# Router gates on GpSimd, a shared tail tile for two batches, and a new instruction order in a fused pooled-attention and mixture-of-experts kernel

## The chip, the cores and the metric

The kernel runs on one core of one Trainium2 chip. A core has five engines that run side by side, each through its own queue in order: PE (TensorE, matmuls and transposes into PSUM), DVE (VectorE), ACT (ScalarE), POOL (GpSimd, which also issues the casting loads) and SP (SyncE, which issues DMAs). PSUM has eight banks. The metric is the device time of one execution in microseconds.

## What is computed

Eight batches; q, k and v of shape (8 batches, 8 heads, 576 tokens, 64), float32. First an attention whose keys and values are means over 8 neighbouring tokens (72 pooled keys); its output, 512 wide, goes into four experts, each a causal attention over 576 tokens with head width 64. A router gives each token the two experts with the largest logits.

```python
k_p = k.reshape(B, H, Sp, pool, D).mean(axis=3)
...
attn = np.exp(scores)
attn = attn / (np.sum(attn, axis=-1, keepdims=True) + 1e-09)
x = attn @ v_p                      # then (B, S, H * D)
...
logits = x @ w_gate
topk = np.argpartition(-logits, K, axis=-1)[..., :K]      # K = 2
w = np.exp(sel); w /= w.sum(-1, keepdims=True) + 1e-09
for e in range(E):
    a = softmax(causal(scale * (x @ wq[e]) @ (x @ wk[e]).T))
    out += mask_e * w_e * (a @ (x @ wv[e]) @ wo[e])
```

## The kernel before

Everything is unrolled: the program is a list of short tokens, SEQ, and each token calls one small function that issues one step for one batch. `S00:3@2` is "scores of expert pair 0, key tile group 0, batch 3, into PSUM bank 2"; a trailing `d` puts a copy on DVE (otherwise ACT), and a trailing `p` on a `y` puts its store off to a later `zs` token. Each engine runs its instructions in the order of the list, and a semaphore is waited for wherever data or a buffer requires it. The list was made by a planner; the kernel's text holds only its result, so the place of a token is the plan's order of time.

The steps of one batch, with capitals for PE and small letters for the engine that empties the bank:

- `L` loads q, k or v (line 126, POOL, cast to bf16; three buffers each), `u` transposes q (298, DVE), `PK`/`kc`/`kt` pool the keys, `PV`/`vc` the values.
- `E` and `e` are scores and exps of the pooled attention (331, ACT), `D`, `d`, `x` the sums and their inverse by log and exp (350 and 354, ACT), `O` and `o` the weighted values into xT (368 and 377, DVE).
- `V` and `v` make the experts' values and the router's logits L (copies at 212); `P` and `p` queries and keys; `S` and `s` the causal scores and their exps into etb (497 and 503, ACT); `a` zeroes the diagonal blocks above the diagonal (512 and 520, POOL).
- `g0` to `g9` make the gates: exp of the logits (ACT), a tournament of maxima and minima for the second largest logit, a mask, the sum and its inverse (415 to 445, DVE).
- `B` multiplies etb with the values and a column of ones; `bz`, `bg` and `b` (555, 557, 562, DVE) take the reciprocal, multiply it with the gate and scale the product into osc. `T`/`t` transposes osc through PE, `F` through a DMA on SP, into oT.
- `Y` and `y` give 128 finished tokens (copies into ofin at 212, ACT or DVE; nine ofin buffers); `zs` stores them from SP (lines 621 and 625).

576 tokens are four tiles of 128 and a tail of 64. Two batches of a pair share one place for their tails (`place` 4), so that xT, the values and the outputs of two tails stand in one tile of 128. The B step isn't shared: each batch has products of 128 rows for its tail, half of them unused, as a part of its own (batches 0, 1, 6, 7) or in a part with a main tile (batches 2 to 5, three tiles wide). W0, W1, W2, W3 and W4 load the weights of query, key, value, router and output.

Of the kernel before, what the change touches and what calls it, by code (L numbers as in the profile page):

```python
# [16 lines left out]
ISEQ = mybir.AluOpType.is_equal  # L17
EXP = mybir.ActivationFunctionType.Exp
# [3 lines left out]
def kernel(  # L22
# [65 lines left out]
    ECOLS = 1664  # L88
# [5 lines left out]
    oscs = bufs(4, [128, NTC, 128], BF16, "osc")  # L94
# [100 lines left out]
    def setup_pads():  # L195
        nc.vector.memset(qks[0][:, :, :, S:SPAD], 0.0)
        nc.vector.memset(qks[1][:, 1, :, MAIN - 64 : MAIN], 0.0)
        for t in vaugs:
            nc.vector.memset(t[:, :, :, HD : HD + 1], 1.0)
        for t in etbs:  # L200
            nc.vector.memset(t[:, :, :, 1600:ECOLS], 1.0)
        for h in range(2):
            nc.vector.memset(etbs[1 - h][64 * h : 64 * h + 64, :, :, 1536:1600], 0.0)
# [183 lines left out]
    def small(b, nm, *shape):  # L387
        if (b // 2, nm) not in at:
            at[b // 2, nm] = gtp.tile([128, NPC, *shape], FP32, name=nm, tag=nm)
        return at[b // 2, nm]  # L390
# [6 lines left out]
    def gate(b, step):  # L397
# [11 lines left out]

        if step == 0:  # L410
            nc.scalar.activation(out=tmp("Ex", E), in_=L, func=EXP)
        elif step == 1:
            L2 = L.rearrange("p c (a b) -> p c a b", b=2)
            for nm, op in (("hi", MAXOP), ("lo", MINOP)):
                nc.vector.tensor_tensor(
                    out=tmp(nm, 2, 1), in0=L2[:, :, :, 0:1], in1=L2[:, :, :, 1:2], op=op
                )
        elif step == 2:
            for nm, src, op in (("s2", "hi", MINOP), ("s3", "lo", MAXOP)):
                nc.vector.tensor_tensor(  # L420
                    out=tmp(nm, 1), in0=got(src)[:, :, 0, :], in1=got(src)[:, :, 1, :], op=op
                )
        elif step == 3:
            nc.vector.tensor_tensor(
                out=tmp("m2", 1), in0=got("s2"), in1=got("s3"), op=MAXOP
            )
        elif step == 4:
            nc.vector.tensor_tensor(
                out=tmp("msk", E), in0=L, in1=got("m2").to_broadcast([128, n, E]), op=ISGE
            )  # L430
        elif step == 5:
            nc.vector.tensor_mul(out=tmp("W", E), in0=got("Ex"), in1=got("msk"))
        elif step == 6:
            nc.vector.tensor_add(
                out=tmp("d2", 2), in0=got("W")[:, :, 0:2], in1=got("W")[:, :, 2:4]
            )
        elif step == 7:
            nc.vector.scalar_tensor_tensor(
                out=tmp("den", 1), in0=got("d2")[:, :, 0:1], scalar=1e-9,
                in1=got("d2")[:, :, 1:2], op0=ADD, op1=ADD,  # L440
            )
        elif step == 8:
            nc.vector.reciprocal(out=tmp("rden", 1), in_=got("den"))
        else:
            nc.vector.tensor_mul(
                out=tmp("G", E), in0=got("W"), in1=got("rden").to_broadcast([128, n, E])
            )
# [88 lines left out]
    def Bv(b, bank, ep, part):  # L536
        p0, p1 = span(b, part)
        for e in range(2):
            for i in range(p1 - p0):
                qc = 4 if p0 + i == 4 else p0 + i - 5 * (b % 2)  # L540
                for c in range(qc + 1):
                    col = EOFF[c] + (qc - c) * 128 - (64 if qc == 4 and b % 2 else 0)
# [3 lines left out]
    def osc(b, ep):  # L546
        return oscs[2 * (b % 2) + ep]

    def bv(b, bank, step, ep, part):
        p0, p1 = span(b, part)  # L550
        own = slice(p0 - 4 * (b % 2), p1 - 4 * (b % 2))
        n = p1 - p0
        o, rz, gt = av(b, bank, part), rzbs[ep][:, :, own, :], gts[ep][:, :, own, :]
# [7 lines left out]
        else:  # L561
            nc.vector.tensor_tensor(  # L562
                out=osc(b, ep)[:, own, :].rearrange("p c (e d) -> p e c d", e=2),
# [5 lines left out]
    def T(b, bank, ep, part=None):  # L569
        p0, p1 = span(b, part) if part is not None else (4 * (b % 2), 4 * (b % 2) + NTC)  # L570
        for i in range(p1 - p0):
            flip(half_bank(bank)[:, 128 * i : 128 * i + 128], osc(b, ep)[:, p0 - 4 * (b % 2) + i, :])

    def t(b, bank, dve, ep, part=None):
        o, oT = b % 2, oTs[2 * (b // 2 % 2) + ep]
        if part is None:
            c0, n, at_ = S * o, S, 64 * o
        else:
            p0, p1 = span(b, part)
            c0, n, at_ = (MAIN + 64 * o, TAIL, 64 * o) if p0 == 4 else (128 * p0, 128 * (p1 - p0), 0)  # L580
        copy(dve, oT[:, c0 : c0 + n], half_bank(bank)[:, at_ : at_ + n])


    def crossbar(b, ep, tail):
        oT, own = oTs[2 * (b // 2 % 2) + ep], osc(b, ep)
        if tail:
            nc.sync.dma_start(out=oT[:, tcols(b)], in_=own[half(b), 4 * (1 - b % 2), :], transpose=True)
        else:
            c = b % 2
            nc.sync.dma_start(out=oT[:, mcols(b)].rearrange("p (c n) -> p c n", n=128), in_=own[:, c : c + 4, :].rearrange("p c n -> p (c n)"), transpose=True)  # L590
# [26 lines left out]
    def z(b, c, queue):  # L617
# [16 lines left out]
        u00:0 L_v1:0 r1:0d w1:0 L_v2:0 u01:0 PK0:0@0 W0:0 kc0:0 PK1:0@1 W1:0 kt0:0d E0:0@24 kc1:0 u10:0 L_k0:1 kt1:0  # L634
        H1:0@0 H1:0@0 e00:0 H1:0@0 L_k1:1 u11:0 H1:0@0 H1:0@0 e01:0 N:0 L_k2:1 E1:0@02 L_q0:1 e10:0 E2:0@46 H1:0@0c
        H1:0@0c H1:0@0c L_q1:1 H1:0@0c e21:0 e20:0 e11:0 D2:0@4 D0:0@5 L_q2:1 PV:0@6 d0:0 D1:0@7 vc:0d H1:0@0 x0:0
        c0:0d L_q3:1 d2:0 O00:0@6 d1:0 c1:0d O20:0@5 O01:0@4 o00:0 O10:0@2 x1:0 O11:0@3 o01:0 x2:0 X0:0@0 W2:0 o10:0
        X1:0 o11:0 X2:0 W3:0 c2:0d X3:0 c3:0d o20:0 P_k0:0@4 L_v0:1 h0:0 P_t0:0@5 p_k0:0d L_v1:1 P_k1:0@3 p_t0:0 L_v2:1
        PK:1@2 p_k1:0 S03:0@0 S00:0@4 kc:1 L_k0:2 S02:0@6 s03:0 s02:0 S01:0@2 kt:1d H1:0@0 L_k1:2 H1:0@0 H1:0@0 s01:0
        H1:0@0 L_k2:2 H1:0@0 u1:1 s00:0 u0:1 a02:0 E1:1@02 L_q0:2 e11:1 E0:1@46 c4:0d H1:0@4c L_q1:2 H1:0@4c e00:1  # L640
        V0:0@2 L_q2:2 V1:0@3 e01:1 a00:0 v0:0d V3:0@4 L_q3:2 v1:0d V2:0@2 e10:1 v3:0d a01:0 D1:1@3 v2:0d L_v0:2 PV:1@4
        d1:1 g1:0 E2:1@06 D0:1@2 vc:1d a03:0 x1:1 H1:0@3 L_v1:2 e20:1 g2:0 O11:1@3 e21:1 g3:0 O10:1@4 d0:1 o11:1 D2:1@5
        O01:1@6 L_v2:2 S10:0@0 x0:1 o10:1 S12:0@2 d2:1 s10:0 o01:1 S11:0@4 O00:1@7 g4:0 PK:2@6 s11:0 o00:1 L_k0:3
        O20:1@0 B01:0@1 kc:2 x2:1 B00:0@7 L_k1:3 g0:0 P_q1:1@4 o20:1 kt:2 bz00:0 bz01:0 s12:0 g5:0 L_k2:3 V2:1@0 g6:0
        g7:0 P_q0:1@6 g8:0 L_q0:3 v2:1 u1:2 p_q1:1 P_t0:1@0 a11:0 u0:2 p_q0:1 E1:2@24 L_q1:3 p_t0:1 g9:0 P_k0:1@6
        bg00:0 a10:0 e10:2 b00:0 bg01:0 L_q2:3 b01:0 V0:1@7 e11:2 p_k0:1d a12:0 E0:2@02 v0:1d B10:0@6 L_q3:3 W4:0 e01:2
        V4:1@4 bz10:0 B11:0@7 bg10:0 L_v0:3 b10:0 e00:2 PV:2@5 v4:1d D1:2@6 bz11:0 L_v1:3 P_k1:1@4 vc:2d d1:2 bg11:0
        b11:0 x1:2 E2:2@02 L_v2:3 D0:2@6 p_k1:1d e21:2 O11:2@7 O01:2@5 d0:2 O00:2@2 o11:2 O10:2@4 L_k0:4 e20:2 PK:3@3
        x0:2 o10:2 S03:1@0 S10:1@6 L_k1:4 s03:1 o01:2 s10:1 S01:1@0 o00:2 L_k2:4 V3:1@4 s01:1 kc:3 V1:1@5 L_q0:4 v3:1d
        S02:1@6 S11:1@2 v1:1 kt:3d S12:1@0 s02:1 L_q1:4 V2:2@4 u1:3 P_q1:2@5 a03:1 u0:3 s11:1 L_q2:4 P_q0:2@6 v2:2d  # L650
        s12:1 a02:1 p_q1:2d S00:1@2 L_q3:4 p_q0:2d g0:1 E0:3@04 s00:1 g1:1 L_v0:4 P_k0:2@6 g2:1 e00:3 g3:1 a12:1 g4:1
        P_k1:2@7 p_k0:2d e01:3 L_v1:4 E2:3@02 g5:1 B12:0@6 g6:1 L_v2:4 g7:1 e20:3 B02:0@4 g8:1 e21:3 bz12:0 T10:0@5
        g9:1 p_k1:2 a10:1 E1:3@02 bg12:0 t10:0d L_k0:5 b12:0 bz02:0 B12:1@5 bg02:0 e11:3 b02:0 PK:4@6 L_k1:5 bz12:1
        bg12:1 PV:3@4 b12:1 e10:3 kc:4 S00:2@2 L_k2:5 D1:3@5 vc:3d B01:1@6 s00:2 L_q0:5 kt:4d B02:1@7 T00:0@4 bz01:1
        V1:2@0 d1:3 bz02:1 L_q1:5 bg01:1 bg02:1 T02:0@1 t00:0d T01:0@2 D2:3@3 x1:3 b02:1 D0:3@5 a11:1 b01:1 O10:3@4
        d2:3 O00:3@7 t01:0d d0:3 L_q2:5 D2:2@6 v1:2d T11:0@3 V0:2@2 t02:0 o10:3 x0:3 a01:1 T12:0@5 V3:2@1 u0:4 L_q3:5
        t12:0 v0:2 O20:2@4 O01:3@5 v3:2 O11:3@0 a00:1 o00:3 t11:0 d2:2 L_v0:5 PV:4@1 o11:3 x2:2 x2:3 E0:4@26 o01:3 vc:4
        a00:2 Y3:0@0 L_v1:5 e01:4 o20:2 P_q1:3@5 y3:0dp e00:4 L_v2:5 T12:1@4 u1:4 B10:1@1 P_k1:3@0 p_q1:3 t12:1d bz10:1
        L_k0:6 bg10:1 E1:4@26 b10:1 p_k1:3 g1:2 P_t0:2@5 L_k1:6 e11:4 g2:2 V0:3@4 p_t0:2d Y2:0@0 e10:4 v0:3d Y1:0@5
# [130 lines left out]
```

## Time and profile before

| | |
|---|---|
| median of 3 runs | 154.78 us (154.6 to 155.67) |
| span of the profiled execution, first to last instruction | 152.5 us |
| median less that span (launch and finish around it) | 2.3 us |
| PE, PE weight loads, DVE, ACT, POOL busy | 140.5, 78.8, 125.9, 135.1, 89.5 us |
| loads and stores | 26.67 MB moved by DMA, mean 175 GB/s |
| mean granted TensorE clock | 0.997 |

The profiled execution has no time of its own beside its span; the runs' median stands 2.3 us above it. A row of the groups reads: line, engine, operation, output from input by the program's names, shapes, count, then busy time in us and mean ns of one, then the engine's idle time ahead of these instructions and what ended it. Matmuls overlap, so their mean ns is longer than the distance from one to the next, and PE's busy time is no measure of how full it is.

### The profile page before, as it was taken

Reading aid. Unit: us, or ns where it says so; the run is one execution under the profiler, and the core shown is the slowest. Engines: PE = TensorE matmul, PEld = TensorE weight load, DVE = VectorE, ACT = ScalarE, POOL = GpSimd, SP = SyncE. Lnnn points to the kernel's source line nnn. Section 1 sums busy time; section 2 is a strip of 40 time slices with the busy share of each in tenths; the row PEclk is TensorE's granted clock in tenths of the full one; section 3 lists DMA queues with packets and bytes.
Section 4 is the critical chain, followed back from the end, with each engine's and each line's share of the span. In section 5 each row is a group of like instructions: output and inputs, shape, how many; then the busy total and the mean of one; then the engine's idle time right before and its main releaser. Section 6 shows DMA issues by size and latency. Waiting matters only on the chain.

```text
span 152.5 us, 5419 instructions
## 1 busy us (share of the span) xinstructions
PE 140.5 (92%) x2101; PEld 78.8 (52%) x2122; DVE 125.9 (83%) x415; ACT 135.1 (89%) x247; POOL 89.5 (59%) x161
## 2 busy tenths in 40 slices
PE   6776998999999999999999999999999999999970
PEld 2323353465554465565546655856356667546640
DVE  1784846899899899899989999999897699888960
ACT  3359479999999999999999999999999899999860
POOL 6998588999688979958998171123300344442300
PEclk9999999999999999999999999999999999999998
DMA  4999999999999999999999931536528241389994
GB/s 126 237 186 181 181 179 178 180 180 181 179 188 180 179 181 182 178 180 182 169 173 176 181 34 39 211 84 208 176 92 325 83 121 25 66 282 306 333 340 134
DMA packets 68890, 26.67 MB, mean 175 GB/s; under 512 B 62720, under 2 KB 64000, under 8 KB 68864
## 3 DMA queue, kind: packets, MB, share of 16 engines
q0 software_dynamic: 57408, 14.72, 97.2%
q1 hardware_dynamic: 11088, 10.88, 22.2%
q10 hardware_dynamic: 368, 0.72, 1.5%
q8 instruction: 16, 0.26, 0.6%
q14 instruction: 10, 0.08, 0.2%
HBM read 30.42 MB, written 9.44 MB: 261 GB/s over the span
## 4 chain that ended last, share of the span: by engine, by line
PE 66%; DVE 11%; DMA 10%; POOL 4%; ACT 3%; issue 2%; DVEq 0%; POOLq 0%
PE psum L221 65%; DMA qraw<-in_q_dram 5%; DMA wst_q<-in_moe_wq_dram 4%; DVE xT L377 4%; ACT etb L503 2%; POOL kraw L126 2%; POOL vraw L126 2%; PE psum L230 1%; DVE qT L298 1%; DVE osc L562 1%; DVE oT L212 1%; POOL qraw L126 1%; DVE vp L212 1%; DVE ofin L212 1%; ACT eta L331 1%
## 5 line engine op out<-in xcount | busy, mean ns | idle before, releaser
L503 ACT ACTIVATE etb<-psum 128x1024 bf16<-128x1024 f32 x48 | 47.2, 1032 | 0.8 <-PE psum L221 0.4
L520 POOL TENSOR_SCALAR_AFFINE_SELECT etb<-etb 128x256 bf16<-128x256 bf16 x64 | 25.7, 412 | 37.2 <-ACT etb L503 36.0
L331 ACT ACTIVATE eta<-psum 96x1024 bf16<-96x1024 f32 (+1 forms) x48 | 36.0, 802 | 1.1 <-PE psum L221 0.4
L221 PEld LDWEIGHTS <-etb 128*128 128x128 bf16 x480 | 18.0, 97 | 6.3 <-issue 3.5
L126 POOL DMA_DIRECT2D qraw<-in_q_dram x30 | 19.7, 662 | 2.5 <-DVE gt L557 0.8
L377 DVE TENSOR_TENSOR xT<-psum,rza 128x512 bf16<-128x512 f32 x32 | 20.2, 681 | 1.0 <-ACT rza L354 0.5
L221 PE MATMUL psum<-wvg,xT 128*128 128x260 bf16 x144 | 20.8, 275 | 0.1
L126 POOL DMA_DIRECT2D kraw<-in_k_dram x25 | 19.0, 765 | 2.3 <-POOLq L774 0.8
L221 PE MATMUL psum<-vaug,etb 128*128 128x65 bf16 x480 | 20.2, 193 | 0.0
L126 POOL DMA_DIRECT2D vraw<-in_v_dram x24 | 18.8, 785 | 2.3 <-PE psum L221 1.4
L221 PE MATMUL psum<-xT,wqp 128*128 128x64 bf16 (+1 forms) x123 | 19.2, 282 | 0.5 <-issue 0.2
L221 PE MATMUL psum<-xT,wkp 128*128 128x64 bf16 (+1 forms) x121 | 18.8, 281 | 0.4
L221 PE MATMUL psum<-wop,oT 128*128 128x512 bf16 (+1 forms) x67 | 17.9, 373 | 0.5 <-DVE oT L212 0.3
L212 DVE CAST qk<-psum 128x512 bf16<-128x512 f32 (+1 forms) x23 | 15.0, 653 | 3.6 <-PE psum L221 3.6
L562 DVE TENSOR_TENSOR osc<-psum,gt 128x256 bf16<-128x256 f32 (+2 forms) x40 | 16.7, 421 | 1.0
L221 PE MATMUL psum<-qk 64*128 64x64 bf16 (+4 forms) x192 | 16.2, 277 | 0.6 <-DVE xT L377 0.2
L221 PEld LDWEIGHTS <-xT 128*128 128x128 bf16 x144 | 12.6, 97 | 6.9 <-issue 3.0
L212 ACT COPY ofin<-psum 128x512 f32<-128x512 f32 (+1 forms) x25 | 14.0, 587 | 1.1 <-PE psum L221 0.9
L298 DVE STREAM_TRANSPOSE qT<-qraw 128x576 f32<-128x576 f32 (+1 forms) x18 | 13.2, 750 | 1.0 <-DMA qraw<-in_q_dram 0.9
L221 PE MATMUL psum<-qT,kpT 32*128 32x64 bf16 (+1 forms) x256 | 12.5, 289 | 1.1 <-DVE qT L298 0.9
L221 PE MATMUL psum<-eta,vp 96*32 96x512 bf16 (+1 forms) x256 | 12.7, 288 | 0.5 <-DVE vp L212 0.5
L221 PEld LDWEIGHTS <-wqp 128*128 128x128 bf16 x128 | 8.4, 97 | 8.4 <-issue 2.3
(79 smaller groups left out, 214.4 us busy)
## 6 DMA issues: line engine op xcount, KB each, us to landing
out_dram<-ofin SPq DMA_DIRECT2D x32, 256.0 KB, 2.9
vraw<-in_v_dram POOLq DMA_DIRECT2D x24, 192.0 KB, 6.7
qraw<-in_q_dram POOLq DMA_DIRECT2D x30, 144.0 KB, 7.0
kraw<-in_k_dram POOLq DMA_DIRECT2D x21, 192.0 KB, 7.5
out_dram<-ofin SPq DMA_DIRECT2D x7, 128.0 KB, 2.4
xT<-in_q_dram ACTq DMA_DIRECT2D x2, 288.0 KB, 4.7
xT<-in_k_dram SPq DMA_DIRECT2D x2, 192.0 KB, 4.9
kraw<-in_k_dram POOLq DMA_DIRECT2D x4, 96.0 KB, 5.2
```

The source lines that it names most:

```text
L126: nc.gpsimd.dma_start(out=dst, in_=src)
L212: (nc.vector.tensor_copy if dve else nc.scalar.copy)(out=out, in_=in_)
L221: nc.tensor.matmul(out=out, lhsT=lhsT, rhs=rhs, start=start, stop=stop)
L230: nc.tensor.transpose(out=out[s], in_=in_[:, s], identity=ident[0:n, 0:n])
L298: nc.vector.transpose(out=dst.rearrange("p (a s n) -> p a n s", s=32, n=n)[:, :, own], in_=src.rearrange("p (a n d) -> p a n d", n=n, d=32 ...
L331: nc.scalar.activation(out=dst, in_=src, func=EXP, scale=ATT_EXP_SCALE)
L377: nc.vector.tensor_tensor(out=xT[:, 2 * got[0][0] + t : 2 * got[-1][0] + t + 1 : 2, m + got[0][1].start : m + got[0][1].stop], in0=psum[:, ...
L503: nc.scalar.activation(out=et[:, ep, :, eo : eo + n], in_=psum[:, bank : bank + 2, 0:n], func=EXP, scale=MOE_EXP_SCALE,)
L520: nc.gpsimd.affine_select(out=blk, in_=blk, pattern=[[0, 2], [1, 128]], compare_op=ISGE, fill=0.0, base=0, channel_multiplier=-1,)
L562: nc.vector.tensor_tensor(out=osc(b, ep)[:, own, :].rearrange("p c (e d) -> p e c d", e=2), in0=o[:, :, :, 0:HD], in1=gt.to_broadcast([128 ...
```

## The change

1. The gates. Steps 1 to 7 and 9 move from DVE to POOL. Where the tournament stood, each pair of experts is compared: for every expert, the number of experts with a larger logit is counted (sixteen differences per token, a comparison, two halvings by addition), and a count below 1.5 keeps the expert. Step 0 stays on ACT and step 8, the reciprocal, on DVE.
2. The tail. `B` of part 2 is made once for a pair: batch 0's tail goes into partitions 0 to 63 of the product and batch 1's into 64 to 127, so that one product, one scaling and one transpose serve both. Parts 0 and 1 are two tiles each for all batches. Both batches' etb have to hold until then. The pad columns of etb and their fill with ones go.
3. The order. All tokens of SEQ are placed anew and the choice between ACT and DVE for copies is made anew: output copies 25 on ACT and 12 on DVE become 18 and 19 (with two halves of the last), value copies 10 and 26 become 17 and 19. In the head, W3 comes ahead of the last loads of batch 1, and warm-up matmuls stand elsewhere. GpSimd's loads reach further into the kernel: the last two come near E2 of batch 6.

```diff
-    ECOLS = 1664
+    ECOLS = 1600
...
-    oscs = bufs(4, [128, NTC, 128], BF16, "osc")
+    oscs = bufs(4, [128, 4, 128], BF16, "osc")
+    otails = bufs(4, [128, 128], BF16, "otail")
...
         elif step == 1:
-            L2 = L.rearrange("p c (a b) -> p c a b", b=2)
-            for nm, op in (("hi", MAXOP), ("lo", MINOP)):
-                nc.vector.tensor_tensor(
-                    out=tmp(nm, 2, 1), in0=L2[:, :, :, 0:1], in1=L2[:, :, :, 1:2], op=op
-                )
+            other = L.unsqueeze(2).to_broadcast([128, n, E, E])
+            pool.tensor_sub(out=tmp("ahead", E, E), in0=other, in1=L.unsqueeze(3).to_broadcast([128, n, E, E]))
         elif step == 2:
...
+            pool.tensor_scalar(out=tmp("ahead", E, E), in0=got("ahead"), scalar1=0.0, scalar2=None, op0=ISGT)
         elif step == 3:
...
+            pool.tensor_add(out=tmp("c2", E, 2), in0=got("ahead")[:, :, :, 0:2], in1=got("ahead")[:, :, :, 2:4])
         elif step == 4:
...
+            pool.tensor_add(out=tmp("c1", E), in0=got("c2")[:, :, :, 0], in1=got("c2")[:, :, :, 1])
         elif step == 5:
-            nc.vector.tensor_mul(out=tmp("W", E), in0=got("Ex"), in1=got("msk"))
+            pool.tensor_scalar(out=tmp("msk", E), in0=got("c1"), scalar1=1.5, scalar2=None, op0=ISLT)
+            pool.tensor_mul(out=tmp("W", E), in0=got("Ex"), in1=got("msk"))
...
     def span(b, part):
-        if 2 <= b < B - 2:
-            return ([(0, 3), (3, 5)], [(4, 7), (7, 9)])[b % 2][part]
-        return ([(0, 2), (2, 4), (4, 5)], [(5, 7), (7, 9), (4, 5)])[b % 2][part]
+        if part == 2:
+            return 4, 5
+        return (2 * part, 2 * part + 2) if b % 2 == 0 else (2 * part + 5, 2 * part + 7)
...
     def Bv(b, bank, ep, part):
         p0, p1 = span(b, part)
+        if part == 2:
+            for e in range(2):
+                for c in range(NTC):
+                    col = EOFF[c] + MAIN - 128 * c
+                    for h in range(2):
+                        mm(av(b, bank, part)[64 * h : 64 * h + 64, e, 0, :],
+                           etbs[h][:, ep, e, col : col + TAIL],
+                           vaugs[b // 2 % 2][:, place(h, c), 2 * ep + e, :], start=(c == 0), stop=(c == NTC - 1))
+            return
...
-        zs2:6 T11:7@6 B12:7@2 t01:7d t11:7 T02:6@4 B02:7@0 zs1:7 y0:7p bz12:7 Y2:7@3 bg12:7 bz02:7 t02:6 bg02:7 Y3:7@1
-        zs0:7 b02:7 y2:7p b12:7 T02:7@0 y3:7p T12:7@2 t02:7d zs2:7 t12:7d Y4:7@2 zs3:7 ya4:7 yb4:7d
...
+        bz11:7 b01:7 zs1:5 y1:6p Y2:6@4 bg11:7 t10:7 t00:7d T01:7@2 b11:7 Y0:7@0 t01:7d T11:7@1 Y1:7@3 t11:7d y1:7dp
+        Y3:7@2 Y2:7@1 B02:7@3 zs0:6 zs1:6 y3:7dp y3:6p y2:6p zs3:6 y0:7p zs2:6 bz02:7 B12:7@0 bz12:7 zs0:7 bg02:7 bg12:7
+        b12:7 y2:7p b02:7 T12:7@1 zs1:7 T02:7@0 t02:7d t12:7 Y4:7@2 zs3:7 yb4:7d zs2:7 ya4:7
```

More of the change, by code (lines that the diff above doesn't have):

```diff
@@ L17 @@
 ISEQ = mybir.AluOpType.is_equal
+ISGT = mybir.AluOpType.is_gt
+ISLT = mybir.AluOpType.is_lt
 EXP = mybir.ActivationFunctionType.Exp
@@ L388, in small @@
         if (b // 2, nm) not in at:
-            at[b // 2, nm] = gtp.tile([128, NPC, *shape], FP32, name=nm, tag=nm)
+            at[b // 2, nm] = gtp.tile([128, NPC, *shape], BF16 if nm in ("ahead", "c2") else FP32, name=nm, tag=nm)
         return at[b // 2, nm]
@@ L408, in gate @@
         L = got("L")
+        pool = nc.gpsimd
         if step == 0:
@@ L562, in bv @@
             nc.vector.tensor_tensor(
-                out=osc(b, ep)[:, own, :].rearrange("p c (e d) -> p e c d", e=2),
+                out=osc(b, ep, part).rearrange("p c (e d) -> p e c d", e=2),
                 in0=o[:, :, :, 0:HD],
@@ L698 @@
[L698 to L701 removed]
+        u00:0 L_v1:0 r1:0d w1:0 L_v2:0 u01:0 PK0:0@0 W0:0 kc0:0 PK1:0@0 W1:0 kt0:0d kc1:0 u10:0 E0:0@24 H1:0@1 e01:0
```

195 lines of the change are left out of this document (87 added, 108 removed).

## The prediction

> **What bounds the kernel now.** I read the page's first two parts, then busy time by stretch of the span, then the chain of waits, then the groups of ScalarE, VectorE and GpSimd.
>
> ```profile
> span 152.5 us, 5419 instructions
> ...
> PE 140.5 (92%) x2101; PEld 78.8 (52%) x2122; DVE 125.9 (83%) x415; ACT 135.1 (89%) x247; POOL 89.5 (59%) x161
> ...
> ACT  3359479999999999999999999999999899999860
> POOL 6998588999688979958998171123300344442300
> ...
> DMA  4999999999999999999999931536528241389994
> GB/s 126 237 186 181 181 179 178 180 180 181 179 188 180 179 181 182 178 180 182 169 173 176 181 34 39 211 84 208 176 92 325 83 121 25 66 282 306 333 340 134
> ```
>
> A slice is 3.8 us. Three things are to be seen: ACT is at 9 from slice 7 to slice 33; DMA is full at a flat 180 GB/s until slice 23 (the loads) and once more, at 282 to 340 GB/s, in the last four full slices (the stores); POOL is nearly full exactly as long as the loads last. By stretch (engines in the order PE, PEld, DVE, ACT, POOL; then granted clock, DMA share, GB/s):
>
> ```profile
> 24.00:36.00 12.00, 11.46 (x177) 6.17 (x178) 10.03 (x32) 11.65 (x21) 11.51 (x19) 1.00 1.82 180
> 36.00:49.00 13.00, 12.65 (x179) 6.71 (x177) 12.21 (x32) 12.69 (x22) 10.74 (x19) 1.00 1.77 182
> 49.00:62.00 13.00, 12.80 (x226) 7.03 (x227) 12.16 (x43) 12.67 (x29) 11.83 (x21) 1.00 1.82 180
> ...
> 133.00:148.60 15.60, 14.58 (x188) 8.79 (x188) 13.04 (x57) 13.82 (x27) 3.60 (x9) 1.00 0.91 312
> 24.00:148.60 124.60, 121.85 (x1871) 70.61 (x1888) 111.74 (x373) 120.58 (x224) 70.32 (x131) 1.00 1.18 175
> ```
>
> The last row less the one above it: from 24 to 133 us ACT works 106.8 of 109.0 us, 98%. PE shows 98% too, but its ends are modelled; the clock is 1.00. I take ACT as the clock of the middle: what leaves ACT leaves the time, unless another limit stands right behind. The two ends have other clocks. From the chain:
>
> ```profile
> 15.00 8.13 DMA qraw<-in_q_dram
> ...
> 23.21 0.79 DVE qT L298
> ...
> 148.16 0.42 DVE ofin L212
> ```
>
> The head ends when the last q piece of batch 1 lands (issued at 15.00, landed at 23.1); nothing of ACT's matters before. The last copy ends at 148.6, and 3.9 us of store and finish follow it up to the span's 152.5. The median, 154.78, lies 2.3 us above this span; I make the sum on the span and add it to the median.
>
> **The change, part by part.** *Gates.* Ten VectorE instructions of each batch go, 80 in all; the reciprocal stays. The ten groups, first and last of them:
>
> ```profile
> L445 DVE TENSOR_TENSOR G<-W,rden 128x16 f32<-128x16 f32 (+1 forms) x8 | 1.8, 221 | 0.2
> ...
> L420 DVE TENSOR_TENSOR s<-hi 128x4 f32<-128x4 f32 (+1 forms) x8 | 1.3, 156 | 0.0
> ```
>
> They add to 15.7 us of DVE (80 by 0.196). DVE isn't the clock, so by itself this is worth nothing: ACT hides it. It is worth what ACT hands over to DVE, which ends near 114 us of work with that.
>
> *ACT.* Counting each engine's instructions in the two programs, ACT loses 7 output copies (24 to 17), 4 large and 2 small query/key copies, one wide one (in the head), one 256 and four 64 wide oT copies; it gains 7 value copies with their 4-wide logit copies (10 to 17), one 128 wide oT copy and one weight copy in the head.
>
> ```profile
> L212 ACT COPY ofin<-psum 128x512 f32<-128x512 f32 x24 | 13.6, 596 | 0.6 <-PE psum L221 0.4 <-ACT oT L212 0.2
> ...
> L212 ACT CAST qk<-psum 128x512 bf16<-128x512 f32 x10 | 5.8, 590 | 0.5 <-PE psum L221 0.5
> ...
> L212 ACT CAST vaug<-psum 128x256 bf16<-128x256 f32 x10 | 3.8, 387 | 0.0
> ...
> L212 ACT CAST qk<-psum 128x256 bf16<-128x256 f32 x5 | 2.0, 408 | 0.3 <-PE psum L221 0.3
> L212 ACT COPY oT<-psum 128x256 bf16<-128x256 bf16 x5 | 1.9, 388 | 0.4 <-PE psum L230 0.4
> L212 ACT COPY L<-psum 128x4 f32<-128x4 f32 x10 | 1.9, 191 | 0.0
> ...
> L212 ACT COPY oT<-psum 128x64 bf16<-128x64 bf16 x4 | 0.9, 218 | 0.0
> ```
>
> By busy time over count (neighbours overlap a little): 7 x 0.57 + 4 x 0.58 + 2 x 0.40 + 0.38 + 4 x 0.22 less 7 x (0.38 + 0.19) less 0.3 is 8.4 - 4.3 = 4.1 us; at ACT's 98%, **-4.2 us** (-3.9 to -4.3). If all of it counted, the last copy would end at 144.4.
>
> *Tail of the order.* In the new order the freed ACT time lies before the end, and 15 output copies come after the last score exp (8 before). I compare what each engine still has to do at one place. Behind the ACT copy y1:5p the new order leaves ACT six output copies, a half one and two oT copies, 4.7 us by the rows above. DVE's rows:
>
> ```profile
> L562 DVE TENSOR_TENSOR osc<-psum,gt 128x256 bf16<-128x256 f32 x24 | 10.1, 420 | 0.5
> L212 DVE COPY ofin<-psum 128x512 f32<-128x512 f32 x11 | 7.3, 683 | 0.0
> ...
> L557 DVE TENSOR_TENSOR gt<-rzb,G 128x4 f32<-128x4 f32 x24 | 4.3, 182 | 0.5
> L555 DVE RECIPROCAL rzb<-psum 128x4 f32<-128x4 f32 x24 | 4.1, 175 | 1.4 <-PE psum L221 1.1
> ...
> L212 DVE COPY oT<-psum 128x256 bf16<-128x256 bf16 x11 | 3.1, 284 | 0.2 <-PE psum L230 0.2
> ...
> L562 DVE TENSOR_TENSOR osc<-psum,gt 128x128 bf16<-128x128 f32 x8 | 2.2, 288 | 0.2
> ```
>
> Behind the same place DVE still has 2.5 output copies (1.8), six oT copies (1.6), six reciprocals (1.1), six gt products (1.1), four wide and two narrow osc products (2.3): 7.8 us, 3.2 more than ACT. In the old order, where ACT has as much left (behind y0:6p, 4.6 us), DVE has 19 instructions, 5.5 us, 0.9 more. So DVE, not ACT, ends the new order, and gives back **+2.3 us** (0 if DVE runs ahead of its place in the order, 3.2 if nothing of the old 0.9 counts).
>
> *Shared tail tile.* One bank with both batches' last 64 tokens replaces two with an idle half. Matmuls stay 480, but 160 now have 64 columns of weights; recip/gt/osc steps stay 40. Eight osc products of 384 columns become 256 wide; four flips and four crossbar transposes go. All of it lies off ACT: 0, with PE's slack and ACT's 98% as the cover. The 160 matmuls cost between half (two halves side by side) and all of an old one:
>
> ```profile
> L221 PE MATMUL psum<-vaug,etb 128*128 128x65 bf16 x480 | 20.2, 193 | 0.0
> ...
> L221 PE MATMUL psum<-eta,vp 96*32 96x512 bf16 x128 | 11.1, 382 | 0.5 <-DVE vp L212 0.5
> ```
>
> The second row shows four 32-column tiles side by side (11.1/128 = 87 ns each where one takes 382), so I take half; the other end is 80 x 42 ns = 3.4 us over the whole span, 0.4 in the last pair.
>
> *Head.* The small gate-weight load now stands ahead of batch 1's last k and q pieces: its issue plus a 4 KB transfer, **+0.2** (0 to 0.7, the price of a whole issue).
>
> *Loads.* GpSimd's loads go through one full queue at 180 GB/s, so the n-th can't land earlier than now, whatever ACT does.
>
> ```profile
> 43.22 2.37 POOL L126 DMA_DIRECT2D kraw<-in_k_dram  x3
> ...
> kraw<-in_k_dram POOLq DMA_DIRECT2D x21, 192.0 KB, 7.5
> ```
>
> Loads 45 to 47 (batch 4's k) are issued from 43.2 on and land 7.5 us later, by 52.3. New loads 46 and 47 (the last k of batch 4 and v of batch 3) no longer have wop ahead of them (256 KB, 1.4 us at 180 GB/s): 50.9 at best. By ACT's clock the new order wants them at 50.7, some 2.8 us earlier than the old one. The queue thus takes part of the lead: **+0.4** (0 to 0.9). What is late next is batch 3's pooled v, and with it ACT's exps.
>
> *GpSimd.* It gets 80 small instructions, 20 of them between 24 and 62 us. Nothing like them is in the trace; the nearest rows:
>
> ```profile
> L520 POOL TENSOR_SCALAR_AFFINE_SELECT etb<-etb 128x256 bf16<-128x256 bf16 x64 | 25.7, 412 | 37.2 <-ACT etb L503 36.0 <-PE psum L221 0.5
> L126 POOL DMA_DIRECT2D qraw<-in_q_dram x30 | 19.7, 662 | 2.5 <-DVE gt L557 0.8 <-DMA wst_q<-in_moe_wq_dram 0.7 <-DVE kf L278 0.5
> L126 POOL DMA_DIRECT2D kraw<-in_k_dram x25 | 19.0, 765 | 2.3 <-POOLq L774 0.8 <-issue 0.7 <-DVE xT L377 0.2
> ...
> L181 POOL IOTA diff<- 128x128 f32 x1 | 0.3, 253 | 0.1
> L774 POOL MEMSET const-bfloat16-1.0<- 128x1 bf16 x1 | 0.1, 101 | 0.0
> ```
>
> The price lies between 0.10 us (one element) and 0.41 (256); the gates have 4 to 80, so I take 0.25, the row of 128. In that stretch the new POOL order holds 17 q and 20 k/v issues, wop and 17 selects, 32.6 us at these rows, and 20 x 0.25 = 5.0, together 37.6 of the 37.5 that ACT's clock gives it: just full. It costs **0**, because loads stand eight deep in the queue (7.5 us from issue to landing) and masks wait for that long less often; without that cover, at 0.41, it costs 3.3. Behind each waiting gate step on POOL stand loads and masks, behind a mask PE's products; VectorE's reciprocal (step 8) stands between two POOL steps and holds DVE's queue while it waits.
>
> The Trainium skill (GPSIMD Engine Reference, section 4.1, Engine selection) speaks against the move: elementwise work with two inputs is about twice as slow there as on VectorE. By that, as an estimate, the 0.196 of the DVE groups becomes 0.39, and 20 of them overfill the stretch by 2.9 us. No run here shows the rate yet.
>
> *Stores.* The next row gives 13 stores in 9.8 us, 0.76 each, at the GB/s of the last slices.
>
> ```profile
> 138.10 9.83 SPq L625 DMA_DIRECT2D out_dram<-ofin  x13
> ```
>
> The new order has 23 stores from y4:3 on, 17.4 us; ACT then has 13.0 us left, and with the 3.2 of DVE 16.2. So the store queue adds up to 1.2 (2 if the end is quicker): **+0.6**.
>
> *Sum:* -4.2 + 2.3 + 0.2 + 0.4 + 0 + 0.6 = -0.7 us; span 151.8, time **154.1 us**.
>
> **The rivals.** (1) *ACT's relief counts in full.* DVE and PE run ahead of the order, stores keep up: -4.2 + 0.2, span 148.5, 150.8 us. For it: DVE has 13 us free between 24 and 148.6. Against: DVE still waits for PE's last products, and DMA is at 0.91 in the last stretch. (2) *GpSimd becomes the bound between 24 and 62 us*, the other side. At 0.41 a gate step its queue is 3.3 us too long, masks and then loads come late and ACT idles: -0.7 + 3.3, 157.4 us. It decides above about 0.29 us each (0.7/20 over my 0.25). For it: POOL works 34.1 of 38 us there already; against: the steps are small, and a late load has 7.5 us of queue ahead of it anyway.
> By the factor of two that the Trainium skill gives (GPSIMD Engine Reference, section 4.1), as an estimate, this rival would come at -0.7 + 2.9, 157.0 us.
>  (3) *The stores end it:* at 282 GB/s, the slowest of the full slices, 23 stores take 21.4 us, 5.2 beyond the work: 154.1 + 4.6 is 158.7; with 306 GB/s 156.9. For it: the slices; against: 340 in the last full one.
>
> **How the numbers follow.** Forecast 0.53 (152.7 to 155.8: give-back 0.9 to 3.2, loads and stores at their bounds), rival 1 0.24 (150.8 to 152.7), rival 2 0.15, rival 3 0.08. The range 151.6 to 156.8 leaves out the lower half of rival 1 and the upper part of 2 and 3. About 1% (1.5 us) is what a measurement of this kernel can tell from no change: faster (below 153.2) is rival 1 and the edge of the forecast, 0.29; slower (above 156.3) most of rivals 2 and 3, 0.21; the rest 0.50.
>
> **What would show it.** In the profile after: ACT busy near 130.5 (135.1 less 4.1 and the wide copy's 1.0, plus a weight copy) and DVE near 114 us; ACT at 9 until some 15 us before the end, then gaps released by DVE or by PE; POOL groups of gate steps near 0.25 us; POOL at 9 up to 62 us without idle time of masks behind it; kraw and vraw as releasers of PE near 50 us; GB/s above 330 in the last four slices. I am wrong if ACT idles before 60 us behind POOL (rival 2), if SP issues run on without data to wait for (rival 3), or if ACT stays full to the end (rival 1).

## The result, and the profile after

| | before | after |
|---|---|---|
| median of 5 runs each, side by side | 154.6 us (154.33 to 155.67) | 159.68 us (159.48 to 162.06) |
| ratio, 95% interval | | 1.0335 [1.0292, 1.0379] |
| span of the profiled execution | 152.5 us | 158.9 us |

The changed kernel is slower by some 5.1 us; the forecast was 154.1 us in a range that ended at 156.8. One execution here (162.06 us) and one of the run with narrow products below (160.84 us) were slower ones at a lower mean clock (0.979 and 0.973), and the ratios leave them out. The profiled execution took 160.69 us, about 1 us above the median, so the differences of spans below come out 1.3 us larger than the medians' difference. Within one and the same execution the time stands some 1.7 us above the span (160.69 and 158.9; 154.28 and 152.5 for the kernel before), not the 2.3 that the median less the profiled span suggested. First the page of the changed kernel: span, busy times, and the rows of ScalarE, GpSimd and DMA by slices of 4 us.

```profile
span 158.9 us, 5378 instructions
...
PE 144.1 (91%) x2118; PEld 76.7 (48%) x2118; DVE 117.5 (74%) x332; ACT 131.4 (83%) x244; POOL 108.6 (68%) x241
...
ACT  3369368997899887969999899999999999978540
POOL 6997497989998899768799899304381825937000
...
DMA  4999999999999999999999994972065521399995
GB/s 128 232 184 184 175 180 181 179 170 138 154 156 173 183 105 152 173 183 243 180 182 158 114 99 64 145 123 72 0 190 166 198 60 27 77 320 344 360 381 176
```

ACT's work fell by 3.7 us, nearly as forecast, and yet ACT is below 9 in many slices ahead of the middle, where it was at 9 throughout. The loads, at a flat 180 GB/s before, dip to 138, 154 and 156 in three slices and to 105 and 152 in two later ones, and keep DMA full to the end of slice 24, 95 us, where it was slice 23 of 3.8 us, 88 us. (The 243 of one slice is not loads alone: 124 of it are stores.) And ACT's last slices run down early (7, 8, 5, 4, 0) while the stores fill DMA. So time was lost at two places. The stretch from 24 to 105 us in one row each, the kernel before first; the columns are PE, PEld, DVE, ACT, POOL, then clock, DMA share and GB/s:

```profile
24.00:105.00 81.00, 79.60 (x1289) 44.71 (x1300) 75.08 (x228) 79.43 (x146) 58.82 (x102) 1.00 1.50 163
```

The changed kernel, and three stretches within:

```profile
24.00:105.00 81.00, 75.01 (x1210) 40.99 (x1212) 64.31 (x175) 74.17 (x138) 67.46 (x138) 1.00 1.50 156
...
36.00:49.00 13.00, 11.50 (x163) 5.78 (x162) 10.97 (x29) 11.35 (x22) 12.46 (x22) 1.00 1.58 152
49.00:62.00 13.00, 12.21 (x224) 6.85 (x224) 10.46 (x29) 11.93 (x25) 11.91 (x27) 1.00 1.54 151
62.00:75.00 13.00, 11.58 (x180) 5.94 (x180) 8.59 (x21) 10.89 (x18) 9.83 (x17) 1.00 1.62 196
```

ACT, the clock of this stretch, idled 1.6 of 81 us before and 6.8 now: 5.3 us more. PE and DVE are emptier as well; POOL alone works more, by 8.6 us. Of the 196 GB/s in the last row 40 are stores; by its own packets the load queue moved 151, 148 and 155 GB/s in the three stretches. The end, from ScalarE's order of time; before, the last wide score exp and the last copy:

```profile
141.25 1.02 ACT L503 ACTIVATE etb<-psum 128x1024 bf16<-128x1024 f32 x1
...
148.04 0.37 ACT L212 COPY ofin<-psum 128x256 f32<-128x256 f32 x1 [0.48 <-PE psum L221]
```

The same two of the changed kernel, whose other half of the last copy is DVE's (at 154.80):

```profile
142.10 1.03 ACT L493 ACTIVATE etb<-psum 128x1024 bf16<-128x1024 f32 x1
...
154.63 0.37 ACT L213 COPY ofin<-psum 128x256 f32<-128x256 f32 x1 [1.12 <-PE psum L222]
```

From the last score exp to the start of the last copy it was 6.9 us (141.25 to 148.16), and is 12.7 (142.10 to 154.80). I call this stretch the end. It is 12.1 us in the profile of the run with the router's weights put back, an execution of 159.44 us, so some 0.6 of the 12.7 can belong to the one execution. ACT's account of the whole span: work -3.7; idle time up to 24 us +1.2 (of it 1.0 the wide copy that went to DVE); 24 to 105 us +5.3; 105 to 135 us -0.4; from 135 us on +4.0. Together +6.4, the difference of the spans.

### The profile page after: what moved, and what is told of

It is laid out like the page before. It is cut to its first block, busy times and chain, and to the rows that moved or that the text cites. A ratio compares the mean times of both kernels' runs of the same rounds, so it can differ in the third digit from the quotient of the medians.

```text
span 158.9 us, 5378 instructions
## 1 busy us (share of the span) xinstructions
PE 144.1 (91%) x2118; PEld 76.7 (48%) x2118; DVE 117.5 (74%) x332; ACT 131.4 (83%) x244; POOL 108.6 (68%) x241
## 4 chain that ended last, share of the span: by engine, by line
PE 34%; POOL 28%; DMA 25%; issue 5%; DVE 3%; ACT 1%; POOLq 0%; ACTq 0%; DVEq 0%
PE psum L222 33%; DMA vraw<-in_v_dram 9%; POOL vraw L129 7%; POOL qraw L129 6%; DMA wst_k<-in_moe_wk_dram 5%; DMA wop<-in_moe_wo_dram 5%; POOL etb L510 5%; DMA qraw<-in_q_dram 4%; POOL kraw L129 3%; DMA out_dram<-ofin 2%; ACT etb L493 1%; DVE xT L378 1%; POOL ahead L419 1%; PE psum L231 1%; POOL etb L502 1%
## 5 line engine op out<-in xcount | busy, mean ns | idle before, releaser
L510 POOL TENSOR_SCALAR_AFFINE_SELECT etb<-etb 128x256 bf16<-128x256 bf16 x64 | 24.8, 408 | 10.5 <-ACT etb L493 10.2
L213 DVE CAST qk<-psum 128x512 bf16<-128x512 f32 (+2 forms) x30 | 19.6, 658 | 5.1 <-PE psum L222 4.8
L222 PE MATMUL psum<-wop,oT 128*128 128x512 bf16 (+1 forms) x74 | 19.6, 382 | 0.4 <-DVE oT L213 0.3
L222 PE MATMUL psum<-xT,wkp 128*128 128x512 bf16 (+1 forms) x128 | 19.3, 286 | 0.0
L222 PE MATMUL psum<-vaug,etb 128*128 128x65 bf16 (+1 forms) x480 | 17.8, 195 | 1.3 <-DVE kf L279 0.6
L222 PEld LDWEIGHTS <-etb 128*128 128x128 bf16 (+1 forms) x480 | 15.4, 102 | 6.9 <-issue 4.8
L213 DVE COPY ofin<-psum 128x512 f32<-128x512 f32 (+1 forms) x19 | 12.3, 673 | 3.5 <-PE psum L222 3.2
L563 DVE TENSOR_TENSOR osc<-psum,gt 128x256 bf16<-128x256 f32 x32 | 13.4, 418 | 0.6
L355 ACT ACTIVATE rza<-rza 128x512 f32<-128x512 f32 (+1 forms) x24 | 12.5, 531 | 0.2
L213 ACT COPY ofin<-psum 128x512 f32<-128x512 f32 (+1 forms) x18 | 9.9, 578 | 3.2 <-DMA out_dram<-ofin 1.5
```

Of the source, the lines that this page charges most:

```text
L213: (nc.vector.tensor_copy if dve else nc.scalar.copy)(out=out, in_=in_)
L222: nc.tensor.matmul(out=out, lhsT=lhsT, rhs=rhs, start=start, stop=stop)
L355: nc.scalar.activation(out=rz, in_=rz, func=EXP, scale=-1.0)
L510: nc.gpsimd.affine_select(out=blk, in_=blk, pattern=[[0, 2], [1, 128]], compare_op=ISGE, fill=0.0, base=0, channel_multiplier=-1,)
L563: nc.vector.tensor_tensor(out=osc(b, ep, part).rearrange("p c (e d) -> p e c d", e=2), in0=o[:, :, :, 0:HD], in1=gt.to_broadcast([128, 2, ...
```

## The experiments

Two theories stood at the start. **P**: the gates on GpSimd hold up its loads and masks, and ACT waits for what comes late. **S**: too many outputs and their stores are left for the end. All times are medians; ratios are to the kernel before, run on the same chip.

| run | kernel it starts from | us | ratio [95%] |
|---|---|---|---|
| gates on VectorE | after | 160.17 | 1.0373 [1.0336, 1.0411] |
| gates left out | after | 155.21 | 1.0041 [1.0018, 1.0063] |
| early gates on VectorE | after | 157.79 | 1.0173 [1.0104, 1.0241] |
| GpSimd for batches 4 and 5 alone | after | 159.96 | 1.0335 [1.0266, 1.0403] |
| gates on GpSimd | before | 165.27 | 1.0692 [1.0646, 1.0739] |
| late gates on GpSimd | before | 157.61 | 1.0174 [1.0119, 1.023] |
| gates left out | before | 154.42 | 1.0014 [0.9981, 1.0047] |
| half of each store | after | 157.95 | 1.0203 [1.0164, 1.0242] |
| five outputs earlier | after | 164.4 | 1.0621 [1.0559, 1.0682] |
| five outputs earlier, early gates on VectorE | after | 161.01 | 1.0388 [1.0319, 1.0457] |
| gates left out, half of each store | after | 153.39 | 0.9919 [0.9889, 0.9948] |
| router weight back | after | 160.28 | 1.0355 [1.0304, 1.0405] |
| last outputs narrow | after | 159.27 | 1.0311 [1.0243, 1.038] |
| last outputs and products narrow | after | 159.17 | 1.0268 [1.02, 1.0336] |
| last outputs and products narrow | before | 154.43 | 0.9982 [0.9951, 1.0013] |

### Gates on VectorE

```diff
-        pool = nc.gpsimd
+        pool = nc.vector
```

> The changed kernel with its eleven pairwise gate steps on VectorE again, nothing else moved. If GpSimd's gate steps hold the loads back (theory P), the 64th load lands by 71 us instead of 76.6, the third pooled-attention block of the middle starts 3 us earlier, and the time falls from 159.7 to 156 to 158 although VectorE gets some 16 us of work back. If the new order itself or its end is the cause (theory S: the last 23 stores), the time stays at 159.5 or rises.

160.17 us: no gain, and theory P's 156 to 158 is missed. The trace says why this is no acquittal of GpSimd. Its rows from 24 to 105 and from 105 to 135 us:

```profile
24.00:105.00 81.00, 76.95 (x1274) 43.06 (x1286) 72.29 (x224) 76.36 (x145) 55.87 (x97) 1.00 1.49 161
105.00:135.00 30.00, 28.16 (x392) 14.83 (x396) 24.84 (x86) 27.94 (x49) 9.81 (x27) 1.00 0.31 89
```

The loads are on time again: the 64th lands at 70.1 us instead of 76.6, as expected. ACT works 76.36 of the 81 us, 2.2 more than in the changed kernel, but from 105 to 135 us it now loses 1.8. VectorE has 127.4 us of work in all, about what it had in the old order; in the new order this costs time. So all gates cost about the same on either engine, by different ways.

### Gates left out

```diff
+        if step >= 0:
+            return
```

> The changed kernel with gate steps 1 to 9 left out: the exp of the logits stands in for the gate, on ACT as before, so no top-2 choice and no normalisation is made. Neither GpSimd nor VectorE has the gates then. P expects the loads on time but for the head and 155 to 156.5 us. S alone expects 158.5 or more, since the stores at the end are as they were.

155.21 us, 4.5 below the changed kernel, as theory P had it. The stretch of 24 to 105 us in this run:

```profile
24.00:105.00 81.00, 78.51 (x1293) 44.05 (x1305) 68.67 (x183) 78.58 (x148) 57.16 (x100) 1.00 1.51 162
```

ACT is back to 78.6, the last wide score exp starts at 136.03, 5.2 us sooner than in the kernel before, and the end still takes 12.2 us. So the gates cost the new order 4.5 us on GpSimd and 5.0 on VectorE (in their pairwise form; the old tournament was not tried in the new order), and without any gates it is no faster than the old order with them.

### Early gates on VectorE, and GpSimd for batches 4 and 5 alone

```diff
-        pool = nc.gpsimd
+        pool = nc.vector if b < 4 else nc.gpsimd
```

> The changed kernel with the gates of batches 0 to 3 on VectorE and those of 4 to 7 on GpSimd. The loads come by then as in the run with all gates on VectorE (the 64th lands near 70 us), and VectorE is spared the later gates. P expects 156.5 to 158.5, lower than either of 159.7 and 160.2; if it is the end that decides, 158.5 to 160.

157.79 us, 1.9 below the changed kernel, as theory P had it. In the stretch of 36 to 49 us the loads are at full rate again:

```profile
36.00:49.00 13.00, 12.05 (x169) 6.35 (x169) 12.00 (x34) 12.22 (x21) 11.99 (x21) 1.00 1.80 179
```

179 GB/s where the changed kernel has 152. The next run puts batches 6 and 7 on VectorE as well (`pool = nc.gpsimd if b in (4, 5) else nc.vector`):

> The changed kernel with only the gates of batches 4 and 5 on GpSimd, all others on VectorE. If the chain of gate steps and masks on GpSimd delays the last batches, 155.5 to 157 (157.8 with 4 to 7 on GpSimd). If not, VectorE's work at the end costs more than the chain: 158 to 159.5.

159.96 us, somewhat above the second of the two ranges: the last two batches' gates are 2 us dearer on VectorE than on GpSimd. The two engines' prices thus depend on the place: for batches 0 to 3, in the load phase, GpSimd is the dearer, for the last two batches VectorE.

### The gates alone, in the old order

The kernel before with the changed kernel's gate function, and nothing else:

```diff
+        pool = nc.gpsimd
...
+            pool.tensor_sub(out=tmp("ahead", E, E), in0=other, in1=L.unsqueeze(3).to_broadcast([128, n, E, E]))
```

> The kernel before, in its own order, with only the gates computed pairwise on GpSimd. P expects later loads and 157 to 158.5 us against 154.6. If GpSimd's steps are hidden, VectorE's relief counts for nothing and the time stays within 154 to 155.2.

165.27 us, dearer by 7 us than theory P had expected. ACT works only 69.65 of the 81 us. The waits of VectorE name a part that the expectation had small:

```profile
DVE rden L434 <- POOL den L432: 12.7, 8, 3.6
```

Eight reciprocals, placed for gates that were done on the same engine, hold VectorE's queue for 12.7 us in all, up to 3.6 at once. How much of the loss is this and how much the loads was not separated. But the place is: with GpSimd for batches 4 to 7 only (`pool = nc.vector if b < 4 else nc.gpsimd`),

> The kernel before, in its own order, with the pairwise gates on VectorE for batches 0 to 3 and on GpSimd for 4 to 7. If what made all gates on GpSimd so slow in this order (165.3) is loads and masks held up in the load phase, most of the 10.6 us goes: 155 to 157.5. If it is VectorE's queue held by the reciprocal that waits for GpSimd's sum, half or more stays: 158 to 161.

157.61 us, just above the first range. 7.7 of the 10.7 us hang on batches 0 to 3, those in the load phase. This doesn't separate the two causes either: of the 12.7 us that VectorE waited, 8.8 go with them. And the old order without gates:

> The kernel before, own order, with the ten gate steps 1 to 9 left out (the exp of the logits stands for the gate). If ACT is the clock there and VectorE's 15.7 us of gates are hidden, as the prediction has it, 153.8 to 154.8 us; if VectorE's gate steps were on the path after all, 149 to 153.

154.42 us, the same as with them. The VectorE work that the prediction costed at nothing by itself was indeed worth nothing, in the old order. (VectorE's busy time falls by 11.5 us, from 125.9 to 114.4; the 15.7 are the sum of the steps' single times, and neighbours overlap.)

### Half of each store, with and without gates

```diff
-            queue.dma_start(out=out[b, 128 * c : 128 * c + 128, :], in_=ofin[:])
+            queue.dma_start(out=out[b, 128 * c : 128 * c + 128, 0:256], in_=ofin[:, 0:256])
```

> The changed kernel with only the first 256 of the 512 output columns stored (the other half of the output is left out). S expects the end to shrink by 3 to 5 us, to 155 to 157, with the last copies no longer waiting for a store. P alone expects 159 or more, since the loads are as late as before.

157.95 us, 1.7 less, not the 3 to 5 of theory S and not the nothing of theory P; the end still takes 11.7 us. Together with the gates left out:

> The changed kernel with gate steps 1 to 9 left out and only the first 256 of 512 output columns stored. With the gates out alone the end from the last score exp to the last copy was 12.3 us, with half stores alone 11.7. If the gate chain and the store queue are two limits of the same length there, the end falls below 10 us and the time to 151 to 153. If PE and the copies behind it are the limit, the end stays at 11.5 us or more and the time at 154 to 155.

153.39 us, 1.8 below the run with gates left out; its end takes 11.3 us. Both the time and the end lie between what the two expectations named. So half of the store bytes is worth 1.7 to 1.8 us in both, of which the end shows about 1.0, and some 11 us of end are something else.

### Five outputs earlier

Five triples of Y, y and zs, of tiles whose oT was long ready, moved forward in the order, with their copies on DVE. One of them, with its neighbours in the list:

```diff
-        bz01:6 T00:6@6 Y1:2@7 bg01:6
...
-        Y0:6@0 y1:2p y1:5p
...
-        b00:7 zs1:2 T10:7@0
...
+        g0:5 Y1:2@7 zs3:1
...
+        d0:7 y1:2dp O20:6@4
...
+        O00:7@0 zs1:2 zs4:1
```

> The changed kernel with five output tiles (product, copy on VectorE, store) moved 20 to 35 us forward in the order: 1 of batch 1, 0, 1 and 2 of batch 2, 2 of batch 3. Nothing else is moved; the gates stay on GpSimd. If the end is what the new order loses (theory S: from the last score exp to the last copy 12.7 us against 6.9 before, with the store queue and PE full), the end shrinks by 2 to 4 us: 156 to 157.7. If only late loads count (theory P), the time stays at 159 to 160, or the earlier products and copies cost what they cost later.

164.4 us. Up to 104 us it runs like the changed kernel; then the middle loses some 4 to 5 us (last wide score exp at 146.5), and the end still takes 12.2. In the stretch of 100 to 140 us PE waits 2.0 us for VectorE's output copies, which it doesn't in the changed kernel; the rest of the loss stays unexplained. Theory S in its simple form, that the outputs need only be placed earlier, falls. The same with the early gates on VectorE:

> The changed kernel with both: five output tiles earlier, and the gates of batches 0 to 3 on VectorE. P and S together expect 153 to 155.5, about the kernel before; P alone 157 to 158.5; S alone 156 to 158.

161.01 us where 153 to 155.5 had been expected: it missed too.

### Router weight back

W3 behind W2, as in the old order:

```diff
-        o00:0 W3:0 o01:0
...
-        p_k0:0 W2:0 p_t0:0
...
+        o00:0 o01:0
...
+        p_k0:0 W2:0 W3:0 p_t0:0
```

> The changed kernel with the load of the router's weights behind that of the value weights again, so that it no longer stands ahead of batch 1's last k and q. If it shifted the loads' turn on the queue, batch 1's first exp comes up to 1 us earlier and the time falls by 0.3 to 1.0; if it only costs its issue, the time stays within 0.3 of 159.7.

160.28 us, against 159.68 within the spread of the runs: the place of this load is not what costs. The other changes of the head were not tried singly.

### What the end is made of

The last 14 whole outputs are copied and stored with a quarter of their columns; then their products have a quarter as well; then the kernel before is treated like that, with its last 7.

```diff
-        n = 256 if last else 512
+        n = 256 if last else 128 if (b, c) in TAIL_OUT else 512
...
-            copy(dve, ofin[:], psum[:, bank, :])
+            w = 128 if (b, c) in TAIL_OUT else 512
+            copy(dve, ofin[:, 0:w], psum[:, bank, 0:w])
```

> The changed kernel, with the 14 whole outputs that follow its last score exp copied and stored with 128 of their 512 columns (the rest of these outputs is left out); their products in TensorE stay whole. Store theory: half the stores were worth 1.7 us, so with these out of the way 157.5 to 158.2 us and no more. Copy theory (ScalarE's and VectorE's copies set the end): 14 copies lose some 0.38 us each on two engines, 155 to 156.8. Product theory (TensorE sets the end) and chain theory (the steps of the last batches one behind the other, gate, scaling, flip, product, copy): 157.3 or above.

159.27 us. Neither the copies of ScalarE and VectorE nor the stores alone set the end: ACT lost 2.9 us of work between 142 and 151 us and the end is 11.7 us long. (That it is above the run with half of each store, 157.95, stays unexplained; the two intervals just miss each other, at 1.0242 and 1.0243.) The row for that stretch, first of the changed kernel:

```profile
142.00:151.00 9.00, 8.95 (x125) 5.50 (x121) 7.62 (x31) 6.70 (x15) 3.89 (x14) 1.00 0.98 353
```

and of the run with narrow outputs:

```profile
142.00:151.00 9.00, 8.87 (x135) 5.54 (x133) 6.54 (x29) 3.79 (x14) 3.44 (x12) 1.00 0.65 209
```

PE still works 8.87 of 9.00 us, while ACT is at 3.79 and DMA at 0.65. PE's busy time is no measure of how full it is, but the chain of waits of this run consists of PE's steps alone from 146.94 to 150.94 us.

> As in the run with narrow outputs, and the output products of these 14 have 128 columns as well (28 matmuls of 0.38 us that become 0.1 to 0.2). Product theory: another 2 to 4 us less than the run with narrow outputs, 153 to 155.5. Copy and chain theories: within 0.7 us of the run with narrow outputs.

159.17 us, 0.1 below the last run and 0.7 by the ratios, as the chain theory has it, though 28 of PE's products have 128 columns instead of 512. The profiled execution took 160.84 us, the other three 158.40 to 159.54, so I read its shape alone, at 145 to 148 us:

```profile
145.00:148.00 3.00, 1.99 (x36) 1.57 (x36) 2.17 (x12) 0.50 (x3) 2.02 (x7) 1.00 0.79 281
```

PE, relieved, idles a third of the time in this profile. The chain of waits has other work in its place:

```profile
145.22 0.73 POOL etb L510 x2
145.95 0.07 issue
146.03 0.26 POOL d L430
...
146.59 0.19 DVE rden L433
...
146.85 0.23 POOL G L435
...
147.11 0.47 DVE gt L558 x2
```

A mask, batch 7's last gate steps, its reciprocal and the first scaling stand one behind the other. The chain of the run with five outputs earlier, an execution of 164.48 us, has the same steps from 149.40 to 151.76 us. With the gates left out there are no gate steps, and the end is still 12.2 us: there the chain runs through a store (138.92 to 143.59 us) and four ACT output copies behind it, to 146.10. So at least three limits lie close together: PE's products, the last batch's chain, and the stores with ACT's copies. Taking one away took 1.0 us or less off the end.

> The kernel before, with the 7 whole outputs that follow its last score exp copied, stored and multiplied with 128 of their 512 columns (the rest of these outputs is left out). If the end costs by the output work that is placed behind the last exp, 7 outputs here are worth half of what 14 are worth in the changed kernel: with 4 us there, 152.5 to 153. If the old end is a chain of dependent steps: within 0.5 us of the kernel before.

154.43 us: in the old order the width of the last outputs costs nothing; its end is 6.9 us with them whole or narrow.

## Why the prediction was wrong, step by step

**The gates on GpSimd, costed at 0: this step failed, and it holds 4.5 of the 5.6 us between forecast and median.** The price of a step was right. The dearest four groups of gate steps in the changed kernel, by form:

```profile
L419 POOL TENSOR_SCALAR ahead<-ahead 128x80 bf16<-128x80 bf16 x4 | 1.7, 418 | 0.2
L419 POOL TENSOR_SCALAR ahead<-ahead 128x64 bf16<-128x64 bf16 x4 | 1.6, 390 | 0.1
L417 POOL TENSOR_TENSOR ahead<-L 128x80 bf16<-128x80 f32 x4 | 1.3, 320 | 1.9 <-DVE L L213 1.9
L417 POOL TENSOR_TENSOR ahead<-L 128x64 bf16<-128x64 f32 x4 | 1.2, 306 | 2.3 <-ACT L L213 2.3
```

All twenty groups add to 20.2 us, 0.25 each, as assumed. But nearly every step uses the result of the one before, and the chain of waits shows what that adds:

```profile
55.00 0.07 issue
55.07 0.22 POOL d L428
55.29 0.08 issue
55.37 0.25 POOL d L430
55.62 0.07 issue
55.69 0.21 POOL den L431
```

0.07 us between two steps, 0.32 a step where no load is issued between them. The prediction had put the point from which rival 2 decides at 0.29, so the rival was in by its own rule. Its sum for the stretch was short as well: 17 q issues, 20 of k and v, wop and 17 selects come to about 34 us by the rows it shows, not 32.6, and with the gates to 39 of 37.5, overfull before any gap. What failed behind it is the sentence "because loads stand eight deep in the queue": a depth of eight covers one late issue, not a lateness that adds up. From 24 to 62 us POOL was nearly full before, and 20 gate steps of 0.25 us came in. The 55th load, wop, was issued at 58.8 us, and in the same order with the gates on VectorE at 53.8: 5.0 us late, the length of the 20 steps. The 64th landed at 76.6 instead of 70.1 (counted in the traces). The load queue's own rate, in steps of 3 us, never rose above 180 GB/s to make it up. The chain of the changed kernel shows one place where that arrives:

```profile
58.77 7.48 DMA wop<-in_moe_wo_dram
...
67.34 7.18 DMA vraw<-in_v_dram
...
74.58 0.78 DVE qT L299
```

The transposition `qT` needs the last q piece of batch 5, which was issued at 65.27 and landed at 74.38 us (the chain puts a load of v in its place). "What is late next is batch 3's pooled v, and with it ACT's exps" named the kind of path rightly, a late load, then PE, then ACT, but not the load: from 24 to 105 us PE waited 2.3 us for transposed q, 0.7 for v (of batch 4) and 0.6 for k. The size was 5.3 us of ACT idle, not 0.4. "I am wrong if ACT idles before 60 us behind POOL" came true: from 36 to 62 us ACT idled 2.7 us, where it was 0.6.

How the 4.5 us divide is not shown. Taking batches 0 to 3 off GpSimd brings the loads back on time and gains 1.9 us, with the same steps then charged to VectorE; the rest can be the later gates' chain, VectorE's waits for GpSimd (2.3 us for G and 1.3 us for the sum) or late loads whose gain VectorE's work eats up.

**DVE's gates, worth nothing by themselves:** right for the old order (154.42 without them), wrong as a property of the gates: in the new order they cost 5.0 us on DVE, in the pairwise form. Work is hidden by an order, and a new order has to hide it anew.

**ACT's relief, -4.2:** right in size. ACT's busy time fell by 3.7, and in the run without gates the last wide score exp came 5.2 us sooner, in part because more output copies stand behind it. That run's 155.21 us lies 1.1 above the forecast's 154.1, so the rest of the sum held but for 1.1 us. Part of that is luck: the end of that run is 5.3 us longer than the old one, where the sum had 2.3 and 0.6, and the earlier exp makes up for some of it.

**The tail, +2.3, and the stores, +0.6:** too small, and the reason incomplete. The step compared what DVE and ACT have left and concluded "DVE, not ACT, ends the new order". It left PE out. From the start of the last wide score exp on the changed kernel has 30 output products, 94 value products (40 of them for the shared tail) and 18 transposes, the old one 16, 46 and 16 (counted in the traces). The pitches (the distance from one start to the next), from the chain of the run with narrow outputs, in pairs:

```profile
147.77 0.43 PE psum L222 x2
148.20 0.11 PE psum L231 x2
```

and 14 value products from the chain of the changed kernel:

```profile
143.25 0.43 PE psum L222 x14
...
148.01 3.53 DMA out_dram<-ofin
...
152.24 0.17 DVE rzb L556
...
154.80 0.42 DVE ofin L213
```

With 0.215 an output product, 0.055 a transpose, 0.031 a value product and half of that for the tail's, PE has, by this estimate, about 9.7 us left in the new order and 5.8 in the old (the last output's four half-wide products counted as whole in both). The difference of 3.9 us stands beside the 5.8 by which the end grew, but it is arithmetic and not a cause that is shown: with most of the output products at a quarter of their width the time fell by about 1 us at most, as the run with narrow products shows. The last 2.6 us (from 152.24) are the shared tail's own chain, from its reciprocals through scaling, transpose and product to the copy. In between an ACT copy waited for a store to free its ofin buffer. Half of the store bytes is worth 1.7 us by two pairs of runs, where the sum had +0.6 for the whole store queue. Which of the limits the end's growth is due to stays open; shortening two of them together was tried only for the gates with the stores, which brought the end to 11.3 us.

**The shared tail tile, half price:** right. In the changed kernel's order of time, 14 whole products and 20 of the tail's:

```profile
146.89 0.59 PE L222 MATMUL psum<-vaug,etb 128*128 128x65 bf16 x14
...
150.69 0.51 PE L222 MATMUL psum<-vaug,etb 128*64 128x65 bf16 x20
```

Fourteen whole ones have a pitch of 0.031 (0.43 by the chain above), so some 0.16 of the 0.59 is the last one's latency; less that, the 20 take 0.35, 0.017 each.

**The head, +0.2:** right by ACT's account (1.2 us more idle time, 1.0 of it moved work); W3 put back gained nothing.

**The rivals.** Rival 2 (157.4) named the cause, and was given 0.15 because its threshold was compared with busy time alone and the queue's depth was counted as cover. Rival 3 (156.9 to 158.7) is true in part: halving the stores gains 1.7 us. Rival 1 is out: ACT's relief was real, but ACT did not stay full, neither in the load phase nor at the end. The two causes came together, and the range had taken them one at a time.

By the Trainium skill (GPSIMD Engine Reference, section 4.1, Engine selection) elementwise work with two inputs is about twice as slow on GpSimd as on VectorE, and with one input GpSimd runs roughly at line rate. The same steps on VectorE, from the run with gates there:

```profile
L417 DVE TENSOR_TENSOR ahead<-L 128x80 bf16<-128x80 f32 x4 | 0.9, 224 | 0.0
...
L435 DVE TENSOR_TENSOR G<-W,rden 128x20 f32<-128x20 f32 x4 | 0.9, 218 | 0.0
...
L419 DVE TENSOR_SCALAR ahead<-ahead 128x80 bf16<-128x80 bf16 x4 | 0.7, 180 | 0.1
```

The trace doesn't bear that rule out at these sizes: with two inputs 320 against 224 ns at 80 elements and 230 against 218 at 20, a factor of 1.4 and 1.05; with one input, 418 against 180 for the comparison of 80 bf16 elements, a factor of 2.3, but 260 against 254 for one of 20 in f32. Its direction, against the move, was right, and its 157.0 us was nearer to the result than the forecast, though not by the factor of two.

## What to carry to other kernels

Treat an engine that also issues the loads as having no free time as long as the loads are rate-bound: count what it gets by pitch in a dependent row (busy time plus the gap), and every microsecond beyond its slack as lateness of all later loads, however deep the queue stands. When an order is planned anew, work that was hidden in the old one is not hidden by right; leaving it out of both orders tells its price in each. At an end, add up what every engine has left behind one common point, PE too, and expect a second and a third limit right behind the first.

## What the runs showed of the hardware

- Dependent steps on GpSimd stand 0.07 us apart, and a comparison of 80 bf16 elements with a constant takes 418 ns there, 180 on VectorE, while steps with two inputs differ by 1.03 (10 elements, 207 and 201 ns) to 1.43 (80 elements, 320 and 224 ns).
- A load stream held up by late issues fell to 152 GB/s in the stretch of 36 to 49 us, where it has 179 with the gates of batches 0 to 3 on VectorE; afterwards it never went above 180 by its own packets, and the 64th load landed 6.5 us later than with all gates on VectorE.
- Stores of half the size took 1.7 us off the time and 1.0 off the end, though DMA stood at 0.98 and 353 GB/s between 142 and 151 us: a full DMA was not the only limit there.
